# Router logits from block transposes on VectorE, and routing a batch in two halves instead of three groups

## The chip, the cores and the metric

The kernel runs on one core of a Trainium2 chip. A core has five engines that run their own instruction streams and wait for each other by semaphores: TensorE (PE in the profile, with its weight loads as PEld), VectorE (DVE), ScalarE (ACT), GpSimd (POOL) and SyncE (SP), which here issues most of the DMA transfers. The metric is the time of one execution in microseconds (us), as the device measures it; for a program on one core it is that core's time.

## The reference

The input x is 8 batches of 2496 tokens with 256 features. A token mixing by a Fourier filter comes first, then a mixture of experts on all 19968 tokens:

```python
X = np.fft.rfft(x, axis=1)
y = np.fft.irfft(X * (filt_r + 1j * filt_i)[None], n=2496, axis=1)

x = y.reshape(19968, 256)
logits = x @ w_gate                      # 256 x 8
expert_idx = np.argmax(logits, axis=1)
probs = softmax(logits)                  # gate weight: the probability of the chosen expert
h = np.maximum(x @ w1[expert], 0.0)      # 256 -> 1024, relu
out = gate[:, None] * (h @ w2[expert])   # 1024 -> 256
```

All in float32. Each token goes to one of eight experts, and no token is dropped.

## The kernel before

**The transform.** 2496 = 39 x 64, so the Fourier transform is done as two short ones, each a matmul with a constant matrix. Stage a transforms along 39 (`stage_a`, constant `tas`), b along 64 and multiplies by the filter (`stage_b`), c transforms back along 64 (`stage_c`), d back along 39 (`stage_d`, constant `tds`). Between the stages the data goes through DRAM (`zd`, `ud`), since each stage needs another dimension on the partitions; batch 0 alone stays on the chip and is turned with matmuls (`turn_z`, `turn_u`).

**Chunks.** In stage d a batch is 22 columns of 117 tokens (three runs of 39 on the partitions; the last column has one run only), with 256 features each. They are handled in six chunks of 4, 4, 4, 4, 4 and 2 columns. `stage_d` (L397) does a matmul of 512 columns for each pair of columns and leaves the result in a y tile of 117 partitions (tokens) by up to 4 columns by 272 values; the last 16 values of a row have room for the token's number and its gate weight. There are six y tiles (`YB`), each held until its rows are scattered; `held_y` counts them, and stage d halts when all are held.

**Logits.** The gate matmul needs the features on the partitions, and y has the tokens there. So `turn_y` (L476) transposes each column's two halves of 128 features with TensorE, four transposes for a pair of columns, into one PSUM bank, and evacuates it to a `yt` tile. When two chunks are there, `logits` (L488) multiplies by `wg`, the gate weights with 8 of 32 columns in use. Four pairs of columns write to four quarters of the partitions of the PSUM tile `lt`, each through one quarter of the PE array's columns. The logits are evacuated to `ls`, turned back to tokens-on-partitions by two more PE transposes (`turn_logits`, L502) and evacuated to `lg`.

**Routing.** `route` (L514) takes the logits of two chunks, 8 columns (the last group has 6), so a batch is routed in three groups. Some fifteen small VectorE operations find the maximum, the expert and its one-hot `oe`, the softmax sum and its reciprocal `sd`. Two matmuls (L554 with a triangular matrix, L555 with ones) count the tokens ahead of each in its expert's list. ScalarE does the exponential and copies the counts out of PSUM. A scan adds the groups' totals, and the row number of each token is cast to `row`. Then POOL writes the token's number and `sd` into the y rows and scatters each column of 117 rows to the experts' lists in DRAM by an indirect DMA (L615).

**Experts.** The lists are worked off in tiles of 512, 256 or 128 rows: SP loads rows and weights, VectorE transposes the rows in blocks of 32 x 32 (`turn_x`, L748), the hidden layer follows (L791 to L804, or L832 to L838), and `result` (L840) multiplies by the second weights, scales by the gate weight and scatters to the output from POOL.

**The order of the work.** PE, DVE, ACT and SP execute in an order that the program fixes when it is built: a planner adds up costs in us (`now`, and `free` for VectorE, ScalarE and POOL) and picks the next step. `slot(k)` (L867) lists for each batch the steps of stages a, b, c, d with a fraction of the slot at which each is due, a cost on PE, and the stream it belongs to. Stage d of batch k-1 lies in slot k, its chunk c due every 0.089 of a slot; logits and routing have due times of their own (L897 to L904). Between these steps the planner sets expert work by a credit. Evacuations from PSUM (`evac`, L233, recorded at L234) go to VectorE or ScalarE, whichever `free` says is earlier. `route` and the tile maps are generators, worked off a few instructions at a time between the steps (`sides`, `side`).

Of the kernel before, what the change touches and what calls it, by code (L numbers as in the profile page):

```python
# [19 lines left out]
P = 128  # L20
# [18 lines left out]
FT = F // P  # L39

# [13 lines left out]
def dft_tables():  # L54
# [26 lines left out]
    valid = np.zeros((NB, N1, NG))  # L81
    for j in range(NB):
        for i in range(len(range(j, N2, NB))):
            ids[j, :, i] = token(q, NB * i + j)
            valid[j, :, i] = 1.0
# [8 lines left out]
        "td": td.reshape(TK, TP),  # L94
        "sg": np.concatenate([sg[:, :NF // 2], sg[:, NF // 2:]]),
        "ids": ids.reshape(TP, NG),
        "valid": valid.reshape(TP, NG),
# [23 lines left out]
def kernel(  # L121
# [52 lines left out]
    tau0 = perm.tile([1, 64], F32, name="tau0")  # L174
# [12 lines left out]
    tds = cst.tile([TK, TP], F32, name="tds")  # L187
# [4 lines left out]
    CT = 32  # L192
    wg = cst.tile([P, DH, CT], F32, name="wg")
    tri = cst.tile([TP, TP], F32, name="tri")
    ones = cst.tile([TP, P], F32, name="ones")

    WM = 8
# [4 lines left out]
    vld = cst.tile([TP, NG], F32, name="vld")  # L202
    e_i = cst.tile([P, E], I32, name="e_i")
# [4 lines left out]
    tau_i = pro.tile([1, 64], I32, name="tau_i", bufs=1)  # L208
# [57 lines left out]
    def load_rest():  # L266
        nc.sync.dma_start(out=tds, in_=td)
        nc.vector.memset(wg, 0.0)
        nc.sync.dma_start(out=wg[:, :, :E], in_=moe_w_gate.rearrange("(i p) e -> p i e", p=P))
        nc.sync.dma_start(out=ids0, in_=ids)  # L270
        nc.sync.dma_start(out=vld, in_=valid)

    def make_constants():
# [3 lines left out]
            out=tri, in_=ones[:, :TP], compare_op=ALU.is_gt, fill=0.0, base=0, pattern=[[1, TP]], channel_multiplier=-1  # L277
        )
        nc.gpsimd.memset(seg, 1.0)
# [3 lines left out]
        nc.gpsimd.iota(tau_i, pattern=[[1, 64]], base=0, channel_multiplier=0)  # L283
# [17 lines left out]
    ins, outs, lgs, yts, lands = {}, {}, {}, {}, {}  # L301
# [95 lines left out]
    def stage_d(b, c):  # L397
        if c == 0:
            lgs[b] = sb.tile([TP, NG, E], F32, tag="lg", name="lg")
# [3 lines left out]
        yo = outs["o", b, c] = sb.tile([P, 4, DR], F32, tag="y", name="yo", bufs=YB)[:TP]  # L403
        for j in range(0, n, 2):
            p = bank()
            if i0 + j + 2 < NG:
                mm(p[:TP, :], lhsT=tds, rhs=ui[:TK, j:j + 2, :], start=True, stop=True)
            else:

                for i, k in enumerate((TK, NS)):  # L410
                    mm(p[:TP, i * D:(i + 1) * D], lhsT=tds[:k, :], rhs=ui[:k, j + i, :], start=True, stop=True)
            evac(yo[:, j:j + 2, :D], p[:TP, :].rearrange("p (i d) -> p i d", i=2), 512)
# [63 lines left out]
    def turn_y(b, c):  # L476
        yo = outs["o", b, c]
        for j in range(0, CH[c][1], 2):
            pt = bank().rearrange("p (i q) -> p i q", i=4)
            for i in range(2):  # L480
                for dh in range(DH):
                    nc.tensor.transpose(
                        pt[:, 2 * i + dh, :TP], yo[:, j + i, dh * P:(dh + 1) * P], ident[:TP, :TP]
                    )
            yt = yts[b, c, j] = sb.tile([P, 4, TP], F32, tag="yt", name="yt", bufs=4)
            evac(yt, pt[:, :, :TP], 4 * TP)

    def logits(b, g):  # L488

        js = range(min(4, NG // 2 - 4 * g))  # L490
        w = len(js) * CT
        pair = [yts.pop((b, 2 * g + j // 2, 2 * (j % 2))).rearrange("p (i h) q -> p i h q", i=2) for j in js]
        lt = psr.tile([P, 2, E * NG], F32, tag="lt", name="lt")[:, :, :TP]
        for dh in range(DH):
            for j in js:
                mm(lt[j * CT:(j + 1) * CT], lhsT=wg[:, dh, :], rhs=pair[j][:, :, dh, :],
                   start=(dh == 0), stop=(dh == DH - 1))
        ls = sb.tile([P, 2, TP], F32, tag="ls", name="ls", bufs=1)
        evac(ls[:w], lt[:w], 2 * TP)
        outs["l", b] = (g, w, ls)  # L500

    def turn_logits(b):  # L502
        g, w, ls = outs.pop(("l", b))
        n = w // CT
        pt = bank()[:TP, :2 * w].rearrange("p (i w) -> p i w", i=2)
        for i in range(2):
            nc.tensor.transpose(pt[:, i, :], ls[:w, i, :], ident[:w, :w])
        evac(lgs[b][:, 8 * g:8 * g + 2 * n, :].rearrange("p (j i) e -> p i j e", i=2),
             pt.rearrange("p i (j c) -> p i j c", c=CT)[:, :, :, :E], 16 * n)

# [3 lines left out]
    def route(b, c0, c1):  # L514

        t0 = 4 * c0
        w = min(4 * c1, NG) - t0
        lg = lgs[b][:, t0:t0 + w]
        sh3 = (TP, w, E)
        she = (TP, E, w)  # L520

        def small(name, *shape, dt=F32, tag=None):
            n = int(np.prod(shape))
            full = sb.tile([TP, WM * n // w], dt, tag=tag or name, name=name, bufs=1)[:, :n]
# [10 lines left out]
        nc.vector.tensor_tensor(oh, oh, em8[:TP, None, :].to_broadcast(sh3), op=ALU.mult)  # L535
        yield 2
        idx = small("idx", w)
        nc.vector.tensor_reduce(idx, oh, axis=AX.X, op=ALU.min)
        if t0 + w == NG:

            nc.vector.tensor_tensor(idx, idx, vld[:, t0:t0 + w], op=ALU.mult)
        oe = small("oe", E, w)
        nc.vector.tensor_tensor(
            oe, idx[:, None, :].to_broadcast(she), em8[:TP, :, None].to_broadcast(she), op=ALU.is_equal
# [611 lines left out]
```

## Time and profile before

| | us |
|---|---|
| median of 14 runs (1558.05 to 1568.12) | 1562.09 |
| the profiled execution, its own time | 1557.75 |
| its span, first to last instruction | 1556.1 |
| PE busy | 1483.3 (95%) |
| PE weight loads busy | 1166.0 (75%) |
| VectorE busy | 751.2 (48%) |
| ScalarE busy | 479.4 (31%) |
| POOL busy | 697.6 (45%) |

The profile is of one execution. A group line names the source line, engine and operation, the tile written and the tiles read (`out<-in`), the shapes, and the count; after the bar come the busy time in us, the mean duration of one in ns, and the idle time of the engine just before them with what ended it. Matmuls overlap in PE, so their durations add up to more than the busy time. "issue" stands where the engine waited for nothing that the profile shows. The granted clock (PEclk) is the share of full speed that TensorE's throttle gave, 0.983 on average here. The page's line of 40 equal slices shows PE between 70% and 90% in the first quarter of the span and at 90% or more in nearly all later slices.

### The profile page before, as it was taken

To read this page: it belongs to the slowest core of one execution; us is meant where nothing else is said; L and a number is where in the kernel's file an instruction comes from. 1 tells how busy PE (TensorE), PEld (TensorE's weight loads), DVE (VectorE), ACT (ScalarE), POOL (GpSimd) and SP (SyncE) were. 2 spreads that over 40 slices of the span, in tenths; PEclk is the share of its full clock that TensorE was granted. 3 is DMA by queue.
4 is the path that set the end of the run, shared out by engine and by line. 5 is a ranking of instruction groups with operands and counts; after the bars stand their busy time and mean duration, and the time that the engine had idled before them with its cause. 6 is when DMAs were issued, how large, how long until landed. Compare 5 with 4: busy or idle time off the path is not lost. (4 is left out here: it accounts for less than half of the span.)

```text
span 1556.1 us, 23882 instructions
## 1 busy us (share of the span) xinstructions
PE 1483.3 (95%) x7202; PEld 1166.0 (75%) x7202; DVE 751.2 (48%) x1676; ACT 479.4 (31%) x993; POOL 697.6 (45%) x910
## 2 busy tenths in 40 slices
PE   7988897899999999999999999999999999999998
PEld 6543454786567776787777777788888889999997
DVE  4677475425664566555674545457343534440000
ACT  3443342233232233222332223222222222223433
POOL 3343344423635555345635555665455546641111
PEclk9999998999999999999999999999999999999999
DMA  9659898877596548735494446355655443455661
GB/s 239 194 161 290 259 275 234 250 206 240 169 270 178 183 128 240 197 107 167 121 235 115 126 140 158 117 163 145 187 156 187 145 141 113 124 183 169 177 189 39
DMA packets 215174, 276.82 MB, mean 178 GB/s; under 512 B 124228, under 2 KB 162509, under 8 KB 215046
## 3 DMA queue, kind: packets, MB, share of 16 engines
q1 hardware_dynamic: 195925, 231.94, 53.4%
q0 software_dynamic: 19120, 43.33, 8.2%
q8 instruction: 61, 1.00, 0.3%
q14 instruction: 68, 0.55, 0.1%
HBM read 195.19 MB, written 80.64 MB: 177 GB/s over the span
## 5 line engine op out<-in xcount | busy, mean ns | idle before, releaser
L795 DVE TENSOR_TENSOR hT<-bank,hT 128x512 f32<-128x512 f32 (+1 forms) x504 | 300.5, 628 | 322.9 <-PE bank L791 207.0
L849 PE MATMUL bank<-w2t,hT 128*128 128x256 f32 x1984 | 447.1, 383 | 3.9 <-ACT hT L799 3.5
L849 PEld LDWEIGHTS bank<-w2t,hT 128*128 128x128 f32 x1984 | 379.5, 192 | 71.2 <-issue 13.9
L855 POOL DMA_INDIRECT out_dram<-ys,ng x161 | 162.0, 1006 | 466.3 <-ACT ys L854 117.7
L799 ACT ACTIVATE hT<-hT 128x1024 f32<-128x1024 f32 (+1 forms) x144 | 132.5, 956 | 329.1 <-DVE hT L795 325.2
L615 POOL DMA_INDIRECT rows<-yo,row x176 | 178.1, 1012 | 75.1 <-issue 54.4
L791 PE MATMUL bank<-xT,w1t 128*128 128x256 f32 (+1 forms) x864 | 191.9, 358 | 0.4 <-DVE hT L795 0.4
L854 ACT ACTIVATE ys<-bank,ng 128x256 f32<-128x256 f32 x137 | 64.9, 474 | 401.8 <-PE bank L849 299.8
L791 PEld LDWEIGHTS bank<-xT,w1t 128*128 128x128 f32 x864 | 152.0, 191 | 25.8 <-issue 7.1
L791 PE MATMUL bank<-sums,wsum 128*128 128x256 f32 (+1 forms) x576 | 136.9, 360 | 0.4 <-DVE hT L795 0.4
L849 PE MATMUL bank<-w2s,hT 128*128 x592 | 132.6, 379 | 0.0
L748 DVE STREAM_TRANSPOSE xT<-xg 128x512 f32<-128x512 f32 (+2 forms) x126 | 57.6, 495 | 145.6 <-PE bank L832 112.6
L832 PE MATMUL bank<-xT,w1t 128*128 128x128 f32 (+1 forms) x864 | 124.3, 299 | 1.8 <-DVE xT L748 1.8
L832 PEld LDWEIGHTS bank<-xT,w1t 128*128 128x128 f32 x864 | 114.1, 191 | 13.0 <-issue 7.9
L849 PEld LDWEIGHTS bank<-w2s,hT 128*128 128x128 f32 x592 | 110.3, 190 | 13.8
L791 PEld LDWEIGHTS bank<-sums,wsum 128*128 128x128 f32 x576 | 101.8, 192 | 22.3 <-issue 9.0
L369 DVE TENSOR_TENSOR ys<-bank,ht 128x512 f32<-128x512 f32 x80 | 54.9, 687 | 78.9 <-PE bank L362 65.3
L348 PE MATMUL bank<-fin,tas 117*120 117x512 f32 x154 | 77.7, 624 | 6.4 <-DMA fin<-in_x_dram 5.5
L388 PE MATMUL bank<-ys,tcs 128*128 128x512 f32 x140 | 74.0, 612 | 10.0 <-DVE ys L378 6.8
L766 POOL TENSOR_TENSOR wsum<-w1t 128x256 f32<-128x256 f32 x72 | 52.9, 735 | 60.9 <-PE bank L791 60.1
L838 ACT ACTIVATE hT<-bank 128x128 f32<-128x128 f32 (+1 forms) x206 | 61.5, 299 | 48.5 <-PE bank L832 35.6
L362 PE MATMUL bank<-fin,tbs 128*128 128x512 f32 x140 | 73.5, 613 | 1.7 <-DMA fin<-zd 1.7
(143 smaller groups left out, 1621.5 us busy)
## 6 DMA issues: line engine op xcount, KB each, us to landing
w1t<-in_moe_w_dram SPq DMA_DIRECT2D x126, 512.0 KB
w2t<-in_moe_w_dram SPq DMA_DIRECT2D x68, 512.0 KB
fin<-in_x_dram SPq DMA_DIRECT2D x39, 512.0 KB
fin<-zd SPq DMA_DIRECT2D x70, 256.0 KB
ud<-uo SPq DMA_DIRECT2D x70, 256.0 KB
zd<-zo SPq DMA_DIRECT2D x35, 480.0 KB
fin<-ud SPq DMA_DIRECT2D x35, 480.0 KB
xg<-rows SPq DMA_DIRECT2D x112, 128.0 KB
```

What stands on the lines that cost most here:

```text
L348: mm(p[:TK, :], lhsT=tas, rhs=xt[:TP, j:j + 2, :], start=True, stop=True)
L362: mm(p, lhsT=tbs, rhs=zi[:, j:j + 2, :], start=True, stop=True)
L388: mm(p, lhsT=tcs, rhs=ys, start=True, stop=True)
L615: sc = nc.gpsimd.indirect_dma_start(out=rowsd, out_offset=bass.IndirectOffsetOnAxis(ap=at, axis=0), in_=what, in_offset=None,)
L791: mm(q[:, v], lhsT=left[:, v * P:(v + 1) * P], rhs=right, start=True, stop=True)
L795: nc.vector.tensor_tensor(o, q, a, op=ALU.add)
L799: nc.scalar.activation(o.rearrange("p v r c -> p v (r c)"), q.rearrange("p v r c -> p v (r c)"), AF.Relu)
L832: mm(p[:, :m], lhsT=w1t[2 * i + g][:, dh, fh, v * P:(v + 1) * P], rhs=xts[i][:, dh, :m], start=(dh == 0), stop=(dh == DH - 1))
L838: lambda: nc.scalar.activation(hT, p[:, :m], AF.Relu))
L849: mm(p[:, :D], lhsT=hs[i][k % 4 // 2][:, k // 4, k % 2, j * P:(j + 1) * P], rhs=w2, start=(k == 0), stop=(k == FT - 1))
L854: lambda: nc.scalar.activation(ys, p[:, :D], AF.Copy, scale=gate))
L855: nc.gpsimd.indirect_dma_start(out=out, out_offset=bass.IndirectOffsetOnAxis(ap=gis[i].bitcast(U32)[:, j, :1], axis=0), in_=ys, in_offset= ...
```

## The change

The logits are computed chunk by chunk. VectorE transposes y in blocks of 32 x 32: inside each block tokens and features change places, so that 32 features of one group of 32 tokens come to lie on the 32 partitions of that group. A gate matrix with four copies of the weights on its block diagonal (`wb`, 128 x 32 for each of eight groups of 32 features) then multiplies all four groups of tokens at once, and eight such matmuls add up the 256 features. Each of a chunk's four columns writes one quarter of the partitions of `lt`, so a chunk takes 8 x 4 matmuls of 32 columns. `lt` holds three chunks, and one VectorE block transpose of 128 x 96 turns them back (`turn_logits`). The PE transposes of y, of the logits, and the evacuations of `yt`, `ls` and `lg` are gone.

In this layout the token groups lie on other partitions than in y. So after routing, row numbers and gate weights are put back: VectorE spreads them by a mask (`rx`), four small matmuls with a selecting matrix `sel` move them into place (`pr`), VectorE casts the row numbers and ScalarE copies the gate weights (`gts`), which POOL then writes into the y rows.

`route` takes three chunks, 12 columns, twice a batch. Its first round is due after chunk 4's step, its second where the third was. The steps' costs on PE in the planner change with it.

```diff
+CT = 32
+NJ = D // CT
...
-        "td": td.reshape(TK, TP),
+        "td": np.pad(td.reshape(TK, TP), ((0, 0), (0, P - TP))),
...
-    tds = cst.tile([TK, TP], F32, name="tds")
+    tds = cst.tile([TK, P], F32, name="tds")
...
-    wg = cst.tile([P, DH, CT], F32, name="wg")
-    tri = cst.tile([TP, TP], F32, name="tri")
-    ones = cst.tile([TP, P], F32, name="ones")
-
-    WM = 8
+    wb = cst.tile([P, NJ, CT], F32, name="wb")
+    sel = cst.tile([P, CT], F32, name="sel")
+    msk = cst.tile([P, 4], F32, name="msk")
+    tri = cst.tile([P, P], F32, name="tri")
+    ones = cst.tile([P, P], F32, name="ones")
+
+    RC = 3
+    WM = 4 * RC
...
     def load_rest():
         nc.sync.dma_start(out=tds, in_=td)
-        nc.vector.memset(wg, 0.0)
-        nc.sync.dma_start(out=wg[:, :, :E], in_=moe_w_gate.rearrange("(i p) e -> p i e", p=P))
+        nc.vector.memset(wb, 0.0)
+        for i in range(4):
+            nc.sync.dma_start(out=wb[i * CT:(i + 1) * CT, :, i * E:(i + 1) * E], in_=moe_w_gate.rearrange("(j p) e -> p j e", p=CT))
...
+        nc.gpsimd.memset(msk, 0.0)
+        for i in range(4):
+            at = slice(i * CT, (i + 1) * CT)
+            nc.gpsimd.tensor_copy(sel[at], ident[at, at])
+            nc.gpsimd.memset(msk[at, i:i + 1], 1.0)
...
     def turn_y(b, c):
-        yo = outs["o", b, c]
-        for j in range(0, CH[c][1], 2):
-            pt = bank().rearrange("p (i q) -> p i q", i=4)
-            for i in range(2):
-                for dh in range(DH):
-                    nc.tensor.transpose(
-                        pt[:, 2 * i + dh, :TP], yo[:, j + i, dh * P:(dh + 1) * P], ident[:TP, :TP]
-                    )
-            yt = yts[b, c, j] = sb.tile([P, 4, TP], F32, tag="yt", name="yt", bufs=4)
-            evac(yt, pt[:, :, :TP], 4 * TP)
...
+        n = CH[c][1]
+        ty = outs["t", b, c] = sb.tile([P, 4, D], F32, tag="ty", name="ty")
+        nc.vector.transpose(
+            ty[:, :n].rearrange("p i (j x) -> p i j x", x=CT),
+            outs["o", b, c][:, :n, :D].rearrange("p i (j x) -> p i j x", x=CT),
+        )
+        free["v"] = max(free["v"], now[0]) + 0.1 + n * D / 960
+
+    def logits(b, c):
+
+        n = CH[c][1]
+        ty = outs.pop(("t", b, c))
+        if c % RC == 0:
+            outs["l", b] = psr.tile([P, RC, CT], F32, tag="lt", name="lt")
+        lt = outs["l", b][:, c % RC]
+        for j in range(NJ):
+            for q in range(4):
+                mm(lt[q * CT:(q + 1) * CT], lhsT=wb[:, j, :], rhs=ty[:, q % n, j * CT:(j + 1) * CT],
+                   start=(j == 0), stop=(j == NJ - 1))
+
+    def turn_logits(b, g):
+        lg = outs["g", b, g] = sb.tile([P, RC * CT], F32, tag="lg", name="lg")
+        nc.vector.transpose(lg, outs.pop(("l", b)).rearrange("p c x -> p (c x)"))
+        free["v"] = max(free["v"], now[0]) + 0.25
...
     def route(b, c0, c1):
...
-        nc.vector.tensor_copy(row, rowf)
+        rx = small("rx", 4, 2 * w, tag="ex")
+        nc.vector.tensor_tensor(
+            rx, rs.rearrange("p v t -> p (v t)")[:, None, :].to_broadcast((P, 4, 2 * w)),
+            msk[:, :, None].to_broadcast((P, 4, 2 * w)), op=ALU.mult,
+        )
         nc.vector.tensor_copy(cnt, tot[:, :, w])
         yield 2
+        due = free["v"] + 1.0
+        while now[0] < due:
+            yield "wait"
+        n = min(4 * c1, NG) - t0
+        pr = bank()[:, :2 * w].rearrange("p (g v c) -> p g v c", g=4, v=2)
+        rv = rx.rearrange("p g (v c i) -> p i (g v) c", v=2, i=4)
+        for i in range(4):
+            mm(pr[i * CT:(i + 1) * CT].rearrange("p g v c -> p (g v) c"), lhsT=sel, rhs=rv[:, i], start=True, stop=True)
+        row = sb.tile([P, w], U32, tag="row", name="row", bufs=2)
+        gts = sb.tile([P, w], F32, tag="gts", name="gts", bufs=2)
+        nc.vector.tensor_copy(row.rearrange("p (c g) -> p g c", g=4), pr[:, :, 0])
+        nc.scalar.copy(out=gts.rearrange("p (c g) -> p g c", g=4), in_=pr[:, :, 1])
+        free["s"] = max(free["s"], now[0]) + 0.3
+        yield 2
         for i, yo in enumerate(yos):
...
-            nc.gpsimd.tensor_copy(yo[:, :n, D + 8:], sd[:, 4 * i:4 * i + n, None].to_broadcast(sh8))
+            nc.gpsimd.tensor_copy(yo[:TP, :m, D + 8:], gts[:TP, 4 * i:4 * i + m, None].to_broadcast(sh8))
...
-                if c >= 3 and c % 2:
-                    steps.append((at + 0.01, lambda c=c: logits(k - 1, (c - 3) // 2), None, 0.9, "d"))
                 if 1 <= c <= nch:
-                    steps.append((at + 0.03, lambda c=c: turn_y(k - 1, c - 1), None, 0.22 * CH[c - 1][1], "d"))
-                if c >= 3 and c % 2:
-                    later = at + (0.07 if k == 1 else 0.11)
-                    steps.append((later, lambda c=c: turn_logits(k - 1), None, 0.25, "d"))
-                    steps.append((later + 0.001, lambda c=c: sides.append(route(k - 1, c - 3, min(c - 1, nch))), None, 0.0, "d"))
+                    steps.append((at + 0.03, lambda c=c: turn_y(k - 1, c - 1), None, 0.0, "d"))
+                if 2 <= c <= nch + 1:
+                    steps.append((at + 0.01, lambda c=c: logits(k - 1, c - 2), None, 0.7, "d"))
+                g, r = divmod(c - 1 - RC, RC)
+                if r == 0 and 0 <= g < nch // RC:
+                    later = at + 0.07
+                    steps.append((later, lambda g=g: turn_logits(k - 1, g), None, 0.0, "d"))
+                    steps.append((later + 0.001, lambda g=g: sides.append(route(k - 1, RC * g, RC * g + RC)), None, 0.0, "d"))
```

Stage d writes 128 instead of 117 partitions of y (the constant is padded with zeros), and the other routing operations keep their form at 128 partitions and 12 columns.

## The prediction

> **What bounds the kernel now.** I read the stages first: busy time of each engine in consecutive stretches, with the granted TensorE clock and the share of the DMA engines. In each row the window's length is followed by PE, PEld, DVE, ACT and POOL busy us, the clock, the DMA share and GB/s.
>
> ```profile
> core 0: us, PE busy (x) PEld busy (x) DVE busy (x) ACT busy (x) POOL busy (x), PEclk, DMA share, GB/s
> 70.00:250.00 180.00, 158.85 (x634) 80.95 (x632) 118.92 (x306) 72.38 (x166) 67.95 (x86) 0.96 0.83 245
> 250.00:300.00 50.00, 39.79 (x148) 29.40 (x148) 21.64 (x53) 8.72 (x16) 20.56 (x27) 0.86 0.82 237
> 300.00:1000.00 700.00, 679.45 (x3058) 520.12 (x3058) 382.10 (x814) 209.04 (x398) 335.33 (x437) 0.98 0.62 174
> 1000.00:1556.00 556.00, 546.35 (x3070) 494.34 (x3068) 192.78 (x438) 159.39 (x360) 248.76 (x328) 1.00 0.50 151
> ```
>
> From 300 us on PE is busy 97% of the time, VectorE 55%, ScalarE 30%: what leaves PE there shortens the run. Before 300 us PE is busy 198.6 of 230 us and the DMA engines 82 to 83%: there a shorter PE stream partly ends in waiting for transfers. The logits of batches 0 to 2 lie in that early part (first bursts at 79, 159 and 226 us), those of batches 3 to 7 between 373 and 995 us. After 1000 us the expert tiles run nearly alone, and the change does not touch them.
>
> Then the groups by line and shape, for the work that goes and for the nearest relative of the new transposes:
>
> ```profile
> L482 PE MATMUL bank<-ident,yo 117*128 117x117 f32 x352 | 44.5, 268 | 2.2 <-DVE yo L234 2.2
> ...
> L748 DVE STREAM_TRANSPOSE xT<-xg 128x512 f32<-128x512 f32 x56 | 36.3, 686 | 0.3 <-issue 0.3
> ...
> L234 ACT COPY yt<-bank 128x468 f32<-128x468 f32 x63 | 33.3, 559 | 19.9 <-PE bank L482 10.8 <-issue 4.8 <-PE bank L791 3.1
> ...
> L496 PE MATMUL lt<-yt,wg 128*32 128x234 f32 x352 | 31.3, 382 | 10.6 <-ACT yt L234 6.4 <-DVE yt L234 3.1 <-issue 1.0
> ...
> L234 DVE COPY yt<-bank 128x468 f32<-128x468 f32 x25 | 16.0, 644 | 41.1 <-PE bank L482 28.1 <-PE bank L832 6.4 <-issue 5.8
> ...
> L748 DVE STREAM_TRANSPOSE xT<-xg 128x256 f32<-128x256 f32 x28 | 10.7, 420 | 19.4 <-PE bank L832 19.4
> ```
>
> After the bar stand busy us, then the mean ns of one. For a matmul that mean (268, 382 ns) is latency, and matmuls overlap. The spacing of starts is what PE pays, so I read it from the timeline of PE alone, one logits burst and what stands around it, then a rank pair:
>
> ```profile
> 78.17 1.02 PE L388 MATMUL bank<-ys,tcs 128*128 128x512 f32 x2
> 79.13 1.01 PE L496 MATMUL lt<-yt,wg 128*32 128x234 f32 x16
> ...
> 80.07 1.02 PE L482 MATMUL bank<-ident,yo 117*128 117x117 f32 x8
> 80.92 1.04 PE L469 MATMUL bank<-ident,ut 128*120 128x128 f32 x8
> ...
> 86.31 0.32 PE L554 MATMUL bank<-oe,tri 117*117 117x64 f32 x2
> 86.47 0.39 PE L555 MATMUL bank<-oe,ones 117*128 117x64 f32 x2
> ```
>
> One float32 matmul is two passes here (176 logits matmuls, 352 records). A 512-column pass is 0.43 us (1.02 for two less one duration of 0.59), 0.84 ns a column. The second L388 pass thus ends its columns at 79.03, and the first pass on 32 columns of the array starts 0.10 later. The 16 logits passes run as four waves of four, one in each quarter of the array's columns, 0.20 us a wave (234 columns at 0.84 ns, plus 5 ns). The last wave starts at 79.77 and is through at 79.97, and the next transpose starts 0.10 after that. So a burst costs 1.03 us from 79.03 to 80.07, of which 0.2 is entering and leaving the narrow form. Transposes start 0.10 us apart, and short passes with full weights 0.11.
>
> Last, who waits for whom:
>
> ```profile
> PE bank L554 <- DVE oe L543: 11.3, 8, 2.6
> ...
> PEld lt L496 <- ACT yt L234: 9.2, 6, 3.2
> ...
> PEld lt L496 <- DVE yt L234: 4.0, 2, 3.1
> ```
>
> PE stood 13.2 us before logits because yt was not evacuated, and 11.3 us before rank matmuls.
>
> **The change on PE.** Removed:
> - turn_y's transposes: 352 x 0.10 = 35.2 us.
> - 24 logits bursts x 1.03 = 24.7 us.
> - turn_logits' transposes: 48 x 0.11 = 5.3 us.
> - Rank matmuls: 16 groups instead of 24, four passes each, 8 x 4 x 0.11 = 3.5 us. The wider moving side (96 columns, 0.08 us) stays under the 0.11 that 64 columns cost already.
>
> Together 68.7 us.
>
> Added: 48 bursts of 32 matmuls, 64 passes of 32 columns each, in 16 waves of four. No row shows a pass that short, so I bound it. From below, 0.45 us a burst, since four logits passes start within 0.02 us (7 ns each). From above, 64 x 0.11 = 7.0 us, if each went alone as the rank passes do. By columns a wave is 32 x 0.84 + 5 = 32 ns, about as long as starting its four passes. I take that: these passes use the same quarters as L496's, its nearest row. PE's sequencer does not stand against it: the trace's records show 0.125 us between two of its semaphore instructions with eight PE instructions between them in program order, and 0.167 with 24, about 3.5 ns an instruction. A burst is 16 x 0.032 + 0.2 = 0.71 us, and 48 are 34 us. The new pr matmuls (8 passes, two waves, its own entry and exit) are 0.27 x 16 = 4.3 us. Added 38.4, net -30.3.
>
> A sentence apart: the Trainium skill, TensorE: Matmul & The Clock Gate (§ Wait — 56ns, not 53.3ns?), states that matmul starts never come closer than about 25 ns, however few columns. The 7 ns above contradict it across column quarters; taken for all 64 passes it would make a burst 1.8 us, the added work 91 us, and the change a loss of some 25 us.
>
> **Waits.** The 13.2 us for yt have a shape: the last group's transposes are placed beside the second route, whose VectorE chain waits for ScalarE, and yt's evacuation stands behind it. At 907.01 VectorE begins the sd sums, yt is copied at 909.74, PE resumes at 910.43. In the new order chunk 5 is turned when no route has just begun, but chunk 4 may meet the first one. I take half away: -6.6. The rank wait is 11.3/24 = 0.47 each; 16 rank points and 16 new pr points against 24 add 8 x 0.47 = 3.8.
>
> **VectorE and ScalarE.** 40 transposes of 128x1024 at 1.22 us (686 ns plus twice the 266 ns that 256 columns add from 256 to 512) and 8 at 0.69 are 54 us; the lt transposes, 16 x 0.28, 4.5. Gone: 16.0 of yt, some 3 of ls and lg, and a third of the route's operations (about 90 us by their groups; 16 longer rounds at 4.7 are 75), 15. VectorE +25 net; ScalarE loses 33 of yt and about 12 of others. I cost this at nothing: VectorE idles 318 of the 700 us, most of it waiting for PE; without that cover it is up to 25 us. Copies that the planner may give to either engine move to ScalarE.
>
> **Other steps, at nothing or little.** td and yo widen to 128 partitions: same 512 columns. POOL: 176 scatters as before, three chunks behind one wait; nine more small start-up operations stand ahead of the filter products, which wait 17.7 us for a transfer there. A half holds three of six y buffers, and batches are 67 us apart or more, so stage_d does not halt. SP: three more issues of about 1 us for wb; 768 more 32-byte packets at the queue's mean 68 ns over 16 engines are 3.3 us, between 0 and that. Batch 0's last half scatters 10 columns instead of 6, 4 us later at 1.0 each, in a stage with idle PE. I take 2 us for both, bounds 0 and 8.
>
> **Sum.** -30.3 - 6.6 + 3.8 = -33.1 of PE time. Three eighths, 12.4, fall before 300 us; half of that ends in waits for transfers, +6.2. With the 2 us: -25. The profiled execution took 1557.75 us (span 1556.1), 4.3 under the median of the runs shown. 1557.75 - 25 + 4.3 = 1537; predicted 1537.
>
> **The rivals.**
> - All passes on. The yt waits vanish whole, the early stage gains too, and the low clock after such waits (the passes at 911.4 took 0.80 us against 0.38) goes: -33 - 6.6 - 4 = -44, 1518. For it: those waits made the worst gaps. Against: DMA at 83% early.
> - VectorE sets the pace (slower). Each burst now starts behind a VectorE transpose that stands in order with hT adds and the route, and lt has one buffer: chunk 3's logits wait for the transposition of the first half, placed 0.03 of a slot earlier, about 3 us. It decides from 0.5 us a burst (25/48). With the 3 us of 907 to 910 on half of the 48 it is +72 - 25, 1609; with 1 us on each +48 - 25, 1585. For it: yt did this to PE on 8 bursts with VectorE half idle. Against: transposes are issued two thirds of a chunk ahead.
> - Narrow passes cost more. At 0.06 us a wave a burst is 1.16 us, +22, about 1559, no change; at the L496 average of 0.05 us a pass, 3.4 us, +129. Against: the 7 ns starts.
>
> **How the numbers follow.** Mine 0.56 (1523 to 1552); all passes on 0.13; VectorE 0.18 (0.01 faster, 0.02 same, 0.15 slower); narrow passes 0.13 (0.04 faster, 0.05 same, 0.04 slower). A measurement here tells 0.2%, about 3 us. Faster 0.74, same 0.07, slower 0.19. The range leaves out some 0.04 below 1514 and 0.15 above 1569.
>
> **What would show it.** The burst's 64 lt passes in about 0.5 us with 0.1 before and after; transposes of 1.22 us; PE busy in the mixed stage as high as now; no PE waits for ty over 1 us. I am wrong if waits of PE for ty or lt sum past 25 us, or if a wave takes twice 32 ns.

## The result, and the profile after

The changed kernel takes 1636.88 us (median of 10 runs, 1629.86 to 1643.96), the kernel before 1560.36 us on the same chip: a ratio of 1.0492, 95% interval [1.0473, 1.0512]. I forecast 1537, a gain of 25 us; it is a loss of some 77, and the time lies 100 us above the forecast. The profiled execution took 1636.63 us, its span is 1634.9, its granted clock 0.952.

The stages (busy time of each engine in consecutive stretches, same columns as before):

```profile
core 0: us, PE busy (x) PEld busy (x) DVE busy (x) ACT busy (x) POOL busy (x), PEclk, DMA share, GB/s
70.00:250.00 180.00, 143.90 (x1121) 70.95 (x1122) 109.23 (x221) 52.78 (x111) 46.87 (x64) 0.87 0.75 221
250.00:300.00 50.00, 35.08 (x380) 17.55 (x379) 30.53 (x90) 9.84 (x20) 10.41 (x13) 0.75 0.71 174
300.00:1000.00 700.00, 643.12 (x4289) 488.30 (x4287) 372.70 (x743) 175.50 (x323) 327.75 (x428) 0.95 0.62 174
1000.00:1634.00 634.00, 612.78 (x3476) 549.41 (x3476) 219.80 (x485) 174.09 (x376) 283.98 (x373) 0.99 0.48 144
```

PE is busy 92% between 300 and 1000 us, where it was 97%, and the clock is lower in every stretch. Between 300 and 1000 us VectorE, ScalarE and POOL are busy less than before and the DMA share is the same 0.62: PE stands idle without another engine being full. The logits' groups, the transposes and PE's waits say where:

```profile
L505 PE MATMUL lt<-ty,wb 128*32 128x32 f32 x3072 | 57.3, 208 | 76.5 <-issue 53.4 <-DVE ty L490 14.3 <-DVE lg L510 8.6
L490 DVE STREAM_TRANSPOSE ty<-yo 128x1024 f32<-128x1024 f32 x40 | 49.2, 1231 | 14.4 <-PE lt L505 13.9 <-ACT yo L240 0.4
```

```profile
PE lt L505 <- issue: 53.4, 75, 3.5
PE lt L505 <- DVE ty L490: 14.3, 6, 6.9
PE bank L360 <- DMA fin<-in_x_dram: 12.0, 1, 12.0
PE lt L505 <- DVE lg L510: 8.6, 2, 5.4
...
PE bank L553 <- DVE oe L542: 2.9, 2, 2.0
```

The largest entry is "issue": 53.4 us in 75 pieces in which PE had work, waited for no semaphore that the profile shows, and did nothing ("starving" below). Before, the same entry for the logits was 1.0 us. The timeline of PE alone shows one burst with these gaps and one without:

```profile
157.01 1.88 PE L417 MATMUL bank<-fin,tds 120*128 120x512 f32 x4
158.82 0.58 PE L505 MATMUL lt<-ty,wb 128*32 128x32 f32 x43
159.70 0.22 PE L505 MATMUL lt<-ty,wb 128*32 128x32 f32 x2 [0.29 <-issue]
160.43 0.25 PE L505 MATMUL lt<-ty,wb 128*32 128x32 f32 x4 [0.51 <-issue]
161.87 0.25 PE L505 MATMUL lt<-ty,wb 128*32 128x32 f32 x4 [1.19 <-issue]
...
167.60 0.21 PE L505 MATMUL lt<-ty,wb 128*32 128x32 f32 x1 [1.18 <-issue]
169.26 0.21 PE L505 MATMUL lt<-ty,wb 128*32 128x32 f32 x1 [1.45 <-issue]
...
176.38 0.76 PE L505 MATMUL lt<-ty,wb 128*32 128x32 f32 x64
177.07 1.11 PE L421 MATMUL bank<-fin,tds 120*128 120x256 f32 x3
```

The later burst is what I forecast: 64 passes, 0.57 us from the first start to the last, the next work 0.69 after its start. The earlier one starts alike, and after 43 passes comes to one to four passes every 0.72 or 1.44 us; it takes 10.4 us instead of 0.57. What runs beside it is in POOL's timeline:

```profile
157.42 0.99 POOL L631 DMA_INDIRECT rows<-yo,row  x1 [0.30 <-issue]
158.71 0.99 POOL L631 DMA_INDIRECT rows<-yo,row  x1 [0.30 <-issue]
160.01 0.99 POOL L631 DMA_INDIRECT rows<-yo,row  x1 [0.30 <-issue]
...
166.47 0.90 POOL L631 DMA_INDIRECT rows<-yo,row  x1 [0.30 <-DMA rows<-yo,row]
```

These are the routing scatters, about 1 us each, one every 1.29 us. Of the 48 bursts, 17 should by their nominal 0.6 us overlap an indirect DMA of POOL; 15 of these are stalled, by 65.1 us together. The other 31 lose 3.3 us, all in one wait for `ty`. In 11 of the 15 the first gap comes after 40 to 46 passes, in the other four after 21 to 38. (Gaps are summed here from start to start, above 100 ns and less 9 ns each, so the sum is a little larger than that of the idle times.)

Scatters do not slow every short pass. In the trace of the kernel before, the transposes L482 that begin within 1.4 us after the start of a routing scatter follow each other after 102 ns on average, the others after 105; for the logits passes L496, which also use 32 columns of the array, it is 54 and 66 ns. None of those beside scatters waits for "issue". But a burst of L496 has 16 passes, not 64.

Adding up the distances between starts of consecutive PE passes, by what stands in them, gives the whole difference of the two profiled executions. What a pass would take undisturbed has to be assumed from its neighbours, so the rows on waits hold to a few us, the one on the low clock to some ten:

| us on PE | before | after | change |
|---|---|---|---|
| passes at full clock, with entering and leaving the narrow form | 1426.7 | 1408.2 | -18.5 |
| no instruction there, at or inside a logits burst | 1.4 | 71.6 | +70.2 |
| waits for VectorE or ScalarE at logits and `pr` | 15.6 | 26.9 | +11.3 |
| extra time of passes at a low clock | 14.1 | 27.9 | +13.8 |
| other gaps over 0.2 us | 62.3 | 68.0 | +5.7 |
| the rest | 24.4 | 20.3 | -4.1 |

Time under a granted clock of 0.99 grew from 56 to 160 us. That the gaps bring it about is likely and was not tested by itself; in e11 below, which has hardly any issue gaps but longer waits for VectorE, it is 85 us, in e10 38.

### The profile page after: what moved, and what is told of

Read it like the earlier page. It is cut to its first block, busy times and chain, and to the rows that moved or that the text cites. A ratio compares the mean times of both kernels' runs of the same rounds, so it can differ in the third digit from the quotient of the medians.

```text
span 1634.9 us, 28452 instructions
## 1 busy us (share of the span) xinstructions
PE 1493.9 (91%) x9618; PEld 1167.0 (71%) x9618; DVE 768.8 (47%) x1600; ACT 442.3 (27%) x886; POOL 695.2 (43%) x918
## 5 line engine op out<-in xcount | busy, mean ns | idle before, releaser
L807 PEld LDWEIGHTS bank<-xT,w1t 128*128 128x128 f32 x864 | 153.7, 193 | 23.7 <-issue 4.3
L848 PE MATMUL bank<-xT,w1t 128*128 128x128 f32 (+1 forms) x864 | 129.5, 306 | 9.0 <-DMA w1t<-in_moe_w_dram 5.9
L848 PEld LDWEIGHTS bank<-xT,w1t 128*128 128x128 f32 x864 | 117.2, 195 | 21.7 <-DVE xT L764 6.7
L505 PE MATMUL lt<-ty,wb 128*32 128x32 f32 x3072 | 57.3, 208 | 76.5 <-issue 53.4
L865 PEld LDWEIGHTS bank<-w2s,hT 128*128 128x128 f32 x592 | 110.3, 190 | 13.8
L505 PEld LDWEIGHTS lt<-ty,wb 128*32 128x32 f32 x3072 | 43.4, 118 | 106.2 <-issue 73.1
L400 PE MATMUL bank<-ys,tcs 128*128 128x512 f32 x140 | 81.6, 669 | 11.3 <-DVE ys L390 8.6
```

The lines of the kernel that those rows point to most:

```text
L400: mm(p, lhsT=tcs, rhs=ys, start=True, stop=True)
L505: mm(lt[q * CT:(q + 1) * CT], lhsT=wb[:, j, :], rhs=ty[:, q % n, j * CT:(j + 1) * CT], start=(j == 0), stop=(j == NJ - 1))
L807: mm(q[:, v], lhsT=left[:, v * P:(v + 1) * P], rhs=right, start=True, stop=True)
L848: mm(p[:, :m], lhsT=w1t[2 * i + g][:, dh, fh, v * P:(v + 1) * P], rhs=xts[i][:, dh, :m], start=(dh == 0), stop=(dh == DH - 1))
L865: mm(p[:, :D], lhsT=hs[i][k % 4 // 2][:, k // 4, k % 2, j * P:(j + 1) * P], rhs=w2, start=(k == 0), stop=(k == FT - 1))
```

## The experiments

**Splitting, scatters away, other groups.** My first theory was that scatters hold up PE's instructions, and that a burst survives as long as it fits what PE holds ready; the rival was VectorE's lateness. The first of four kernels makes two bursts of 32 passes of each burst. The second replaces the routing scatters with SP's transfers to consecutive rows (it leaves out sorting the rows to their experts). The third routes three groups of two chunks again, and the fourth does the logits of two chunks in one burst, with one large `ty` tile and no second one.

```diff
# e1_split
-                    steps.append((at + 0.01, lambda c=c: logits(k - 1, c - 2), None, 0.7, "d"))
+                    for h in range(2):
+                        steps.append((at + 0.01 + 0.04 * h, lambda c=c, h=h: logits(k - 1, c - 2, h), None, 0.35, "d"))
# e2_after_static, in scatter()
-        sc = nc.gpsimd.indirect_dma_start(out=rowsd, ...)
+        sc = nc.sync.dma_start(out=rowsd[filled[0]:filled[0] + m, :], in_=what)
# e3_groups3
-    RC = 3
+    RC = 2
# e4_joint2: RC = 2, and in logits()
+                   rhs=ty[:, :, q, j * CT:(j + 1) * CT]    # 2 chunks, 64 columns
```

> The changed kernel with each chunk's logits burst cut in two steps of 16 matmuls (32 passes, 64 PE instructions), the second placed 0.04 of a slot after the first, other PE work between them. Theory 1 (PE's instructions are handed out slowly while POOL builds an indirect DMA, and a burst of 128 instructions outruns what PE holds ready): issue gaps inside the bursts fall from 65 us to under 10, and the time from 1637 to 1560 to 1585, 96 entries and exits of some 0.2 us instead of 48 included. Theory 2 (narrow passes are slow whenever a scatter runs, however many there are): the gaps stay at 40 us or more and the time at 1620 or more. Theory 3 (VectorE's order is what costs): waits for ty and lt stay and the time stays above 1615.

> The changed kernel with its 176 routing scatters replaced by plain DMAs of the same rows, issued by SP to consecutive rows, and expert tiles that read consecutive rows; rows so meet other experts than the reference's. Same bursts, same VectorE work, but POOL builds no descriptors for the routing. Theories 1 and 2: the gaps inside bursts that met a routing scatter (15 of the 19 gapped bursts) vanish, 65 us become under 12, and the time falls by 45 to 80 us to 1555 to 1590, less what 176 issues of about 1 us cost SP. Theory 3: 1615 or more.

> The changed kernel with routing in three groups of two chunks again, logits still chunk by chunk (one constant changed). Theories 1 and 2: 48 bursts and 176 scatters as in the changed kernel, gaps of 45 to 85 us, time 1615 to 1655. Theory 3, with the halves as the cause of late VectorE work: waits for ty and lt fall by half and the time to 1590 to 1615.

> Logits of two chunks in one burst, 64 passes of 64 columns instead of twice 64 of 32, three groups. The same VectorE work as in the run with three groups, half the PE instructions for the logits. Theory 1: half as many bursts can meet scatters, gaps fall to 20 to 40 us; a burst runs 16 waves of 58 ns, 0.93 us, so the undisturbed work falls by 24 x (2 x 0.79 - 1.15) = 10 us; time 1575 to 1610. Theory 2: gaps as long as columns times disturbed share, 40 us or more, time 1610 or more. Theory 3: 1615 or more.

Measured: split 1544.83 us, 1.0133 [1.0104, 1.0161]; without scatters 1546.26, 1.0148 [1.0121, 1.0175]; three groups 1543.39, 1.0121 [1.0093, 1.0150]; two chunks in one burst 1565.78, 1.0283 [1.0254, 1.0313]. But this chip ran the kernel before in 1523.85 us, where the first one needed 1560, and its traces have almost no issue gaps in bursts, not even in those that meet scatters. So these runs cannot tell who made the gaps. They say that variants of the change cost 1.2 to 1.5% even where PE gets its instructions in time (the changed kernel itself was not run on this chip), that three groups instead of two halves hardly matter there, and that one late `ty` tile for two chunks costs more (PE waited 45.2 us for `ty` there).

**The same on a chip like the first.** The changed kernel once more, a profile of the kernel before, the split again, and the kernel before with nothing of the change but the routing in two halves of three chunks:

```diff
# e8_halves, on the kernel before
-    WM = 8
+    WM = 12
-                    steps.append((later + 0.001, lambda c=c: sides.append(route(k - 1, c - 3, min(c - 1, nch))), None, 0.0, "d"))
+                    if c > 3:
+                        steps.append((later + 0.001, lambda c=c: sides.append(route(k - 1, 3 * (c // 7), 3 * (c // 7) + 3)), None, 0.0, "d"))
```

> The changed kernel itself once more, on the same chip as the three runs beside it. The run with three groups had bursts just as long and no issue gaps, on a chip where the kernel before takes 1524 us instead of 1560. Theory 1a (the gaps belong to the changed kernel's order: its bursts meet scatter chains): gaps of 45 to 85 us again, and 4 to 6% slower than before. Theory 1b (the gaps belong to the chip that ran it: instructions reach PE more slowly there): gaps under 5 us if this chip runs the kernel before in about 1524 us, 1 to 2% slower than before; gaps again if it takes about 1560.

> The kernel before, for a profile of it on the same chip as the runs beside it. Theory 1b: its time and span follow the chip (about 1524 or about 1560), with the same instructions; what differs between the two is small gaps of PE with no visible cause, or the granted clock. Theory 1a: 1555 to 1565 as profiled first, or a difference that has nothing to do with PE's issue.

> Each burst in two halves of 64 PE instructions, as before, now beside the changed kernel on one chip. Theory 1 in both forms: where the changed kernel has gaps, this has under 10 us of them and is faster by at least 50 us; where it has none, the two agree within 15 us, the extra entries and exits being about 9 us. Theory 2: gaps in both.

> The kernel before with only its routing changed: three chunks at a time, twice a batch, the first round where the second group's was, logits still by PE transposes. Theory 3 (later and longer rounds on VectorE and POOL cost by themselves): 0.8 to 2% slower than before. Otherwise within 0.5% of before, since eight rounds of some 3.7 us fewer on VectorE and 3.5 us fewer on PE are nearly nothing.

Before took 1562.0 us here, the changed kernel 1636.15, 1.0484 [1.0437, 1.0532], with the same gaps (61.3 us in bursts that meet an indirect DMA, 3.3 in the others). The profiled execution of the kernel before took 1560.11 us, with waits like those of its first profile (12.6 us for `oe`; 3.4 for ScalarE's `yt` and 2.6 for VectorE's, where it had been 6.4 and 3.1). The split took 1655.96, 1.0618 [1.0580, 1.0655]: the very program that needed 1544.83 on the other chip. Its half bursts starve too (45.1 us of gaps, 43.6 of them in halves that meet an indirect DMA), some after as few as 2 passes, so halving a burst does not save it. The 40 to 46 passes of whole bursts would fit a reserve of instructions that is not refilled while scatters run; no run tests that. Halves alone took 1543.46, 0.9888 [0.9853, 0.9922]: faster than both kernels, where I had expected no change or a loss.

**Is it the count of instructions?** To the kernel before, at the places where the changed one has its logits, 48 bursts of 64 narrow passes are added whose result nobody reads; or, at the same places, one matmul of 512 columns instead, which is about as much PE time in two passes. Beside them the static kernel of e2 and the changed one run on this chip.

```diff
# e9_narrow_added
+        for j in range(8):
+            for q in range(4):
+                mm(p[q * CT:(q + 1) * CT, :CT], lhsT=ident[:, q * CT:(q + 1) * CT], rhs=ident[:, :CT], start=(j == 0), stop=(j == 7))
# e10_wide_added
+        mm(p, lhsT=ident, rhs=ht[:, 0:2, :], start=True, stop=True)
```

> The kernel before with 48 extra bursts of 64 narrow passes (32 columns, 128 PE instructions each), where the changed kernel has its logits, on constants, into a bank that nobody reads; nothing of VectorE, routing or logits is changed. Theory 1 (the instructions of the bursts are the cost): undisturbed they are 48 x 0.79 = 38 us; on a chip that runs the kernel before in about 1560 us, issue gaps of 30 to 70 us come on top, 1620 to 1670 in all, 4 to 7% slower; on one of about 1524, 1.5 to 3% slower. Theory 3 (VectorE's order): no gaps on any chip, 1.5 to 3% slower.

> The same kernel with one matmul of 512 columns in the place of each narrow burst, two passes and four PE instructions, 0.86 us: the same order of all other work, the same time on PE, 6000 PE instructions fewer. Theory 1: 48 x 0.86 = 41 us and no gaps, 2 to 3% slower on either chip; the difference to the narrow bursts is what instructions cost. Theory 3: the two agree within 0.5%.

> The changed kernel with the routing scatters replaced by plain DMAs to consecutive rows from SP, as before, once more for a chip with gaps. Theory 1 with POOL's scatters as what slows the issue: gaps under 12 us on either chip, 1 to 2.5% slower than before. Theory 1 without them (any load): gaps of 30 us or more where the changed kernel has them.

> The changed kernel beside these. On a chip that runs the kernel before in about 1560 us: 4.3 to 5.3% slower, gaps of 55 to 70 us. On one of about 1524: theory 1b gives gaps under 5 us and 1 to 2% slower.

Before took 1561.1 us here. Narrow: 1622.23, 1.0414 [1.0378, 1.0450]; wide: 1567.41, 1.0046 [1.0021, 1.0071]; without scatters: 1552.88, 0.9948 [0.9929, 0.9966]; the changed kernel: 1634.89, 1.0498 [1.0461, 1.0535], with 58.5 us of gaps in bursts that meet an indirect DMA. PE's waits in the narrow kernel, its longest entry:

```profile
PE bank L506 <- issue: 35.3, 55, 1.2
```

13 of the 15 added bursts that meet an indirect DMA are stalled, by 46.3 us. The wide kernel has no such entry. So 55 us come from 128 instructions in a burst where four would do, in the same order of work, with no VectorE transpose in front. (The passes are also narrower. That this alone does it does not fit the narrow L496 passes above, which run freely beside scatters; 64 short passes on the whole array were not tried.) The wide kernel itself was a miss: I had expected 2 to 3%, 41 us, and it cost 0.5%; beside the added work PE's idle time fell from 72.8 to 55.4 us, and the time at a low clock from 56 to 38. Without scatters I had expected a loss of 1 to 2.5%, and it gained 0.5%. And in the changed kernel the gaps vanish with the scatters (3.4 us left in bursts that still meet an indirect DMA):

```profile
PE lt L505 <- DVE ty L490: 24.0, 8, 6.9
PE bank L360 <- DMA fin<-in_x_dram: 14.0, 3, 10.6
PE lt L505 <- DVE lg L510: 13.0, 2, 8.8
...
PE lt L505 <- issue: 1.9, 6, 0.5
```

**Bursts kept away from scatters; the kernel before without scatters.** In e13 the planner holds the logits back from a route's `pr` matmuls to the end of its scatters. e14 takes the scatters from the kernel before, as e2 did (sorting left out).

```diff
# e13_quiet
+        busy[0] = 1e9                     # before pr
...
+        busy[0] = free["p"] + 1.0         # after the last scatter
...
-            return f[2] and f[2][0] in "uy" and held_y[0] == YB
+            return f[2] and (f[2][0] in "uy" and held_y[0] == YB or f[2] == "q" and busy[0] > now[0])
```

> The changed kernel, where the plan doesn't place a logits burst between a route's pr matmuls and the end of the scatters it hands to GpSimd; the bursts, their 64 passes and the 176 scatters stay. Theory 1 (on chips that run the kernel before in about 1560 us, a run of GpSimd's indirect DMAs starves PE of instructions): few bursts meet the routing scatters, issue gaps inside bursts fall from 58 to 65 us to 5 to 20, and the time from about 1636 to 1570 to 1595, the rest above before being waits for VectorE. Rival (the bursts are starved by whatever runs beside them, the routing scatters are just where they happened to lie): gaps of 40 us or more, time 1620 or more. On a chip that runs the kernel before in about 1524 us there are no gaps to save: 1540 to 1550.

> The kernel before, with its routing scatters replaced by SyncE's transfers to consecutive rows (it leaves out sorting the rows to their experts). If the scatters also hold back the kernel before, on a chip of about 1560 us, it gets faster by 5 to 30 us (0.98 to 0.997); if its long passes cover what the scatters delay, as the absence of issue gaps in its logits says, it stays within 0.3%, or gets a little slower by the transfers on SyncE. On a chip of about 1524 us: within 0.5% either way.

> The kernel before with a batch routed in two halves and the logits as they were. It took 0.989 of before on one chip of about 1560 us. If that gain is one of the chip kind (fewer runs of scatters), it is there again at 0.985 to 0.993 on such a chip and within 0.4% of before on a chip of about 1524 us; if it is fewer rank waits and route operations, it is 0.985 to 0.993 on both.

Before took 1562.71 us. Quiet: 1606.55, 1.0284 [1.0241, 1.0328]. The gaps inside and between bursts fell from 68.4 to 26.2 us, 18.9 of them in bursts that still met an indirect DMA, presumably because the planner's clock drifts from the real one; the time fell by 30, less than I expected, while other waits grew (gaps over 0.2 us among other passes rose from 68.0 to 92.2). The kernel before without scatters: 1531.22, 0.9799 [0.9780, 0.9818], just past the large end of my estimate. Here is the surprise: the kernel before has next to no issue gaps in its logits, and still the scatters cost it 31 us. VectorE's "issue" waits, added up over the lines of its waits, fall from 18.5 us in 11 to 4.7 in 4, ScalarE's from 117.7 in 70 to 85.3 in 42, and PE's waits for `oe` and for ScalarE's `yt` nearly go:

```profile
PE lt L496 <- DVE yt L234: 2.6, 1, 2.6
...
PE bank L554 <- DVE oe L543: 1.1, 2, 0.9
PE lt L496 <- ACT yt L234: 1.1, 3, 0.7
```

They were 3.1, 11.3 and 6.4 us. (Gone with the scatters are GpSimd's 176 instructions of about 1 us, their transfers, and the sorting; which of these brings the 31 us was not separated.) Halves again: 1543.66, 0.9876 [0.9855, 0.9897].

With and without scatters, on chips of this kind (each ratio to before in its own runs):

| | with scatters | without |
|---|---|---|
| logits as before | 1 | 0.9799 |
| logits changed | 1.0498 | 0.9948 |

The change costs 5.0% beside scatters and 1.5% without (0.9948 / 0.9799 = 1.015), and its variants cost about as much on the faster chip. So 3.5%, some 54 us of 77, go with the scatters; the gaps in the bursts, 65.1 us in the first trace, and the 55 us between e9 and e10 say that this is the starving. The rest is a loss of 23 us where a gain of 25 was forecast: some 48 us that need another cause.

**The second cause.** In e11, evacuations of y wait for y tiles whose rows are still being written; ScalarE's and VectorE's waits:

```profile
ACT yo L240 <- DMA rows<-yo: 34.4, 8, 10.1
```

```profile
DVE yo L240 <- DMA rows<-yo: 6.7, 2, 4.5
```

Together 41.1 us; in e14, with the logits as before, 2.2. (With scatters the same waits are 14.4 us in the changed kernel and 6.3 in the kernel before, so this stands out only without them.) A late y makes a late `ty`, and behind it on VectorE a late `lg`. So e16 has seven y tiles instead of six; the room comes from one input tile and one tile of gate weights. e17 is its control, without the seventh y tile, and e18 the halves of e8 with the seventh. (e16 and e17 leave out sorting.)

```diff
# e16_static_y7; e18_halves_y7 the same on e8
-    NIN, YB = 7, 6
+    NIN, YB = 6, 7
-        ng = ... name="ng", bufs=8)
+        ng = ... name="ng", bufs=7)
# e17_static_n6: NIN, YB = 6, 6 and bufs=7
```

> The changed kernel without routing scatters (as in the static runs, it leaves out sorting the rows to their experts), with seven y tiles instead of six; to make room, six input tiles instead of seven and seven tiles of gate weights instead of eight. Without scatters it took 1552.9 us where before takes 1561, PE waits for ty and lg were 37 us, and evacuations to y waited 41 us for y tiles whose rows were still being written. Theory 2 (six y tiles are too few for two halves of three: late y, so late ty, so PE waits): the evacuations' waits fall to under 20, PE's waits for ty and lg to under 20, the time to 1530 to 1545. Rival (VectorE's own order is what makes ty and lg late): waits and time as they were, 1550 to 1556. On a chip that runs before in about 1524 us all times are some 7 us lower.

> The control of e16: the same without scatters (sorting the rows left out), six input tiles and seven tiles of gate weights, but six y tiles as in the changed kernel. By theory 2 it is as slow as with seven input tiles, 1550 to 1565, so that the gain of e16 is that of the y tile; if it is as fast as e16, the gain there comes from what loads when.

> The kernel before with a batch routed in two halves, logits as they were, and seven y tiles, six input tiles, seven tiles of gate weights. With six y tiles it took 0.988 of before, and its evacuations to y waited 16 us for y tiles. Theory 2: 0.980 to 0.987; if the y tiles don't matter to it, 0.986 to 0.991; if the input tile is missed, over 0.991.

Before took 1561.64 us. Seven y tiles: 1536.47, 0.9849 [0.9823, 0.9876]; the control: 1557.1, 0.9963 [0.9948, 0.9978]. The seventh y tile is worth 1.1% against the control and 1.0% against e11, 21 and 15 us. The time is as theory 2 (six y tiles are too few) has it, the waits only in part: evacuations still wait 43.7 us for y tiles (61.5 in the control), but PE's waits for `ty` and `lg`, 37.0 us in e11 and 22.8 in the control, are 16.5, all for `ty`:

```profile
PE lt L505 <- DVE ty L490: 16.5, 9, 6.2
```

The control's longest entry is another wait, which e16 does not have, and how much of the 21 us it is by itself was not tested:

```profile
PE bank L374 <- DMA fin<-zd: 19.1, 1, 19.1
```

Halves with seven y tiles: **1532.59, 0.9811 [0.9793, 0.9828]**, against the kernel before the fastest of this study that does all of its work; its evacuations wait 2.9 us for y tiles where e15's waited 15.8. So a seventh tile gives 0.7% with the old logits too: it helps routing in halves, whatever makes the logits. And it isn't the halves alone that make y late. With three groups, in e3 on the faster chip, evacuations still wait 28.6 us for y tiles, in the split with its halves 30.9:

```profile
ACT yo L240 <- DMA rows<-yo,row: 27.6, 8, 7.0
```

```profile
DVE yo L240 <- DMA rows<-yo,row: 1.0, 1, 1.0
```

From the end of a chunk's last evacuation to its first scatter it is 67 us on average in the kernel before, 75 in e3, 83 in e8 and 85 in the changed kernel: the halves lengthen it, and so does something else in the change, since e3 has the groups of before. Which of them costs the time stays open, and the kernel of e14 with a seventh tile was not run.

## Why the prediction was wrong

**The step that failed: "PE's sequencer does not stand against it".** I took 3.5 ns an instruction from two distances between semaphore instructions; they differ by 0.042 us for 16 instructions, which is 2.6 ns. Undisturbed bursts come near either: 64 passes, 128 instructions with their weight loads, in 0.57 us are 4.4 ns each. Beside a run of scatters it is one to four passes in 0.72 us, after some 40 at the undisturbed pace, and this cost 65.1 us in the first trace where I had put nothing. The rows that I read could not show it: the longest row of narrow passes there is 16, and a 512-column pass occupies PE for 0.43 us with two instructions. I asked what the passes cost by columns and by starts, and not what keeps 128 instructions coming. The rival "narrow passes cost more" ended on the right side for another reason: its passes were to be slow always, and they are fast or starved.

**The burst itself** was right in its size: 0.57 us of starts for 16 waves (I had 0.51), and 0.22 around them (I had 0.2). The Trainium skill, TensorE: Matmul & The Clock Gate (§ Wait — 56ns, not 53.3ns?), has matmul starts at least 25 ns apart; in this trace 64 passes over four column quarters start 9 ns apart, so weighing the row above the rule was right. Net of waits PE saved 18.5 us, not 30.3; the bursts, 0.08 us longer each than forecast, are 3.8 of the difference, and the rest was not followed up.

**"A half holds three of six y buffers ... stage_d does not halt", at nothing.** A tile is free only when its rows have landed, and the evacuations into it waited for that. I looked at how many tiles a half holds, and not at how late it gives them back: a chunk's tile waits for the group's last logits, the route, `pr` and the scatters. Without scatters one tile more gave back 15 to 21 us; with them this was not tried on the changed logits.

**VectorE.** Its transposes took 1.231 and 0.69 us (1.22 and 0.69 forecast) and 265 ns for `lt` (280). Its busy time rose by 18 us (25). I cost this at nothing; waits for VectorE or ScalarE at logits and `pr` rose by 11.3 us. In the first profile PE's waits for `ty` and `lg` are 22.9 us, just under the 25 that I named as my bound, without scatters 37.0. The rival "VectorE sets the pace" had the right wait, but it came with six y tiles and went in part with seven (37.0 in e11, 16.5 in e16), so VectorE's order is not all of it.

**The early stage.** I gave 6.2 us of the gain to waits for transfers. PE's waits for the input x are 17.0 us in the changed kernel (12.0 of them one wait) and 9.6 in e6, so the size was about right; that most of it is one wait makes this luck in part.

**Rank and yt waits.** I took half of 13.2 us for `yt`, but that is what the weight loads waited; PE's own wait was 9.5 (6.4 and 3.1). I added 3.8 us for rank and `pr` waits; they fell, from 11.3 to 5.0. e8, where the rank waits fell to 2.0, shows that this comes with the halves: by themselves, with PE logits, they gain 1.1 to 1.2%. The change contained one good edit and one bad one, and I did not price them apart.

## What to carry to other kernels

Before replacing a few long instructions by many short ones, ask what else runs beside them: a busy time that adds up is worth nothing if the instructions don't come, and a trace with long passes and short bursts alone cannot show that they won't. When a step holds a buffer for a larger group, price the time until it is given back (the group's last member, the chain behind it, and the store's landing), not the number held, and test the price: here one tile more paid, but the waits that should explain it went only in part. Test the parts of a change apart: here routing in halves with one more y tile runs at 0.981 of the kernel before, while the whole change runs at 1.049.

## What the runs showed of the hardware

- On chips that run the kernel before in about 1561 us, PE comes to a few passes per 0.72 us while POOL issues indirect DMAs back to back (15 of 17 bursts). What holds the instructions back was not shown: no semaphore in the trace releases PE at the end of such a gap. The instruction packets of queue q8 (16 KB each, 1.07 us in the median; 80 of them, 61 in the kernel before, so taken to be PE's) do not line up with them: none falls into the stalled bursts that begin at 254.63 and 416.12 us; the Trainium skill, Runtime: NRT & Kernel Launch (§ Instruction fetch mechanics), holds fetch to be hidden because an engine issues more slowly than it is filled, and whether 4.4 ns an instruction is too fast for that was not tested. Nor is it known whether a run without profiling has them, since every run here was measured with its spans.
- It is not PE alone: VectorE's and ScalarE's "issue" waits fell by 13.8 and 32.4 us when the kernel before lost its scatters, and its time by 31 us.
- One chip ran the kernel before in 1523.85 us, and a program that took 1655.96 elsewhere in 1544.83. The two kinds of chips lie 38 us apart in the kernel before, and it loses 31 us to its scatters on the slower kind, so the scatters may make most of the distance. That is not shown: the kernel before without scatters was not run on the faster one, and why that one's PE does not starve stays open.
